# Spectral mixing and two expert layers on one Trainium2 core: split and transpose of a slot's rows two slots ahead

## The chip, the core and the metric

The kernel runs on one core of a Trainium2 chip. The metric is the device time of one execution in microseconds; the median of three runs before the change is 3485.12 us (3482.34 to 3485.62). Five engines work side by side: TensorE (PE, with its weight loads listed as PEld), VectorE (DVE), ScalarE (ACT), GpSimd (POOL) and SyncE (SP), which here issues DMAs only. Each engine takes its instructions in the order in which the program lists them.

## The reference

What is computed, cut to what matters:

```python
X = np.fft.fft(np.fft.fft(x, axis=1), axis=2)      # x: 8 x 3072 x 256
x = X.real.reshape(24576, 256)
h = x @ w_in                                       # 256 -> 2048
x = softplus(h) @ w_out                            # 2048 -> 256
xn = x / (norm(x) + 1e-6); en = emb / (norm(emb) + 1e-6)
logits = xn @ en.T / tau                           # 8 experts
e = argmax(logits); gate = softmax(logits)[e]
out = gate * (relu(x @ w1[e]) @ w2[e])             # 256 -> 1024 -> 256, expert e of each row
```

## The kernel before, in words

**First stage** (until about 2330 us of the span). The transform and the dense layer run as one software pipeline over 256 units (batch, tile, quarter of the features). A router gives each finished row an expert, and POOL scatters the rows into `bucket` in DRAM, sorted by expert (line 960).

**Second stage.** `phase2` (it works under the name P2) runs 104 slots of rows that share one expert. A slot has 256 rows, as two tiles of 128 rows; the last 8 slots have one tile. All matmuls use f16 pairs (a high and a low part), so each product is three matmuls. One slot j is made of these steps, and each step is a small function:

- `p2_load` (line 1126): SP loads the slot's rows `r` from `bucket`, four buffers. A load waits until the scatter of the slot that last used the buffer has landed.
- `p2_norm` (lines 1144 to 1170), a generator with four parts. Part 1: ACT squares and sums the rows (`jk`, line 1144), POOL takes the root (`nr`, line 1147). Part 2: DVE makes the power-of-two scales `s2` of the slot (lines 1150 to 1155). Part 3: DVE lines 1157 to 1160, then ACT's exponentials `lg` (line 1164). Part 4: DVE makes the output scale `gm` (lines 1167 to 1170).
- `p2_wcopy` (line 1135): from slot 19 on, DVE copies the expert's weights out of the table `W` into one of three buffers `wb`; the copy takes 2.30 us.
- `p2_split` (lines 1179 and 1180): DVE scales the rows by `s2` and splits them into a high and a low f16 part `xs`. There is one buffer `xs`.
- `p2_tr` (line 1187): SP issues one DMA that transposes `xs` into `xT`, of which there are two buffers.
- `p2_m1` (line 206 under the names `psH<-xT,wb`), called for the two halves of the features: 24 matmuls each, ACT takes relu of the sums to `hh` (line 1209), DVE the rest to `hl` (line 1210).
- `p2_m2`: 48 matmuls `psO<-wb,hh` and `psO<-wb,hl` with `hh` and `hl`, ACT scales the result to `ot` (line 1233), POOL scatters it to the output (line 1235).

The order in which a slot's turn lists them is written out by hand: load of row j+3; first half of m1(j); split and transpose of slot j+1; second half of m1(j); norm part 1 of slot j+2; weight copy for j+2; the other parts of that norm; m2(j).

In the turns in which the table `W` is filled, `ahead()` is called three times a turn: a block of zeros to `bucket` (`zt`, line 1113) and three pieces of `W` of 512 KB each (line 1116), all on SP. Of these, two pieces stand ahead of the transpose of a turn and one behind it. After the last unit of the first stage a drain begins, in which steps of P2 (one between two `yield`s) are woven into the remaining work of the first stage, three a pass; after four passes one step goes with each turn of a loop that ends the router and its scatters. The table is opened after that.

Of the kernel before, what the change touches and what calls it, by code (L numbers as in the profile page):

```python
# [142 lines left out]
def fft_moe_moe(ctx, tc, x, w_in, w128, w_out, emb, tau, w1, w2, fa, db, mcs, tid, ident, tri, misc, out,  # L143
# [832 lines left out]
    nslot = EARLY + NPS + E if P2ON else EARLY + 1  # L976
# [130 lines left out]
    def p2_zero(n):  # L1107
        if n < E:
            r0 = SY.value_load(p2["cuu"].bitcast(I32)[0:1, 2, n:n + 1], min_val=0, max_val=E * CAP - 256)
            rows = bucket[ds(r0, 128), :]  # L1110
        else:
            rows = bucket[E * CAP + (n - E) * 128:E * CAP + (n - E + 1) * 128, :]
        SY.dma_start(rows, p2["zt"])

    def p2_weights(e, q):
        SY.dma_start(p2["W"][:, e, q * 2048:(q + 1) * 2048], wsc[e][:, q // 2, q % 2 * 2048:(q % 2 + 1) * 2048])
# [4 lines left out]
    def p2_load(j):  # L1121
        rows = p2["a"].tile([128, 2, RW], F32, tag="r", name="r", bufs=RB)
        r = p2["row0"] + j * SLOT if j < K0 else p2["row1"] + (j - K0) * SLOT if j < EARLY else SY.value_load(p2["ti"][0:1, 1, j - EARLY:j - EARLY + 1],
                                                                 min_val=0, max_val=E * CAP)
        nt = 2 if j < EARLY + NPS else 1
        SY.dma_start(rows[:, 0:nt, :], bucket[ds(r, nt * 128), :].rearrange("(t p) d -> p t d", p=128))
        S2[j] = dict(rows=rows, nt=nt)

    def p2_wcopy(j):
        if j < EARLY:  # L1130
            WB[j] = p2["wb"][0 if j < K0 else -1]
            return
        r = V.value_load(p2["ti"][0:1, 0, j - EARLY:j - EARLY + 1], min_val=0, max_val=E - 1)
        WB[j] = wb = p2["wb"][(j - EARLY) % 3]
        V.tensor_copy(wb.bitcast(I32), p2["W"].bitcast(I32)[:, ds(r, 1), :].rearrange("p o n -> p (o n)"))
# [38 lines left out]
    def p2_split(j):  # L1174
        rows = S2[j]["rows"]
        xs = p2["a"].tile([128, 2, 2, 256], F16, tag="xs", name="xs", bufs=1)
        s2 = S2[j]["s2"]
        for t in range(S2[j]["nt"]):
            V.tensor_scalar(xs[:, t, 0, :], rows[:, t, 0:256], s2[:, 0, t:t + 1], None, op0=ALU.mult)
            V.scalar_tensor_tensor(xs[:, t, 1, :], rows[:, t, 0:256], s2[:, 0, t:t + 1], xs[:, t, 0, :],  # L1180
                                   op0=ALU.mult, op1=ALU.subtract)
        S2[j]["xs"] = xs

    def p2_tr(j):
        xs, nt = S2[j]["xs"], S2[j]["nt"]
        S2[j]["xT"] = xT = p2["a"].tile([128, 2, 2, 2, 128], F16, tag="xT", name="xT")
        SY.dma_start_transpose(out=xT[:, 0:nt].rearrange("p t a c n -> p (t a c) n"),
                               in_=xs[:, 0:nt].rearrange("p t a d -> p (t a d)"))

    def p2_m1(j, hf):  # L1190
        d = S2[j]
        wb, xT, nt = WB[j], d["xT"], d["nt"]
        n = nt * 128
        hh = p2["a"].tile([128, 4, 256], F16, tag=f"hh{hf}", name=f"hh{hf}", bufs=1)
        hl = p2["a"].tile([128, 4, 256], F16, tag=f"hl{hf}", name=f"hl{hf}", bufs=1)
        for q in range(4):
            f = 4 * hf + q
            if q % 2 == 0:
                ps = psH[hf % len(psH)].tile([128, 2, 256], F32, tag="H", name="psH", bufs=2)
            i = 0  # L1200
            for c in range(2):
                for a, w in ((0, 0), (0, 1), (1, 0)):
                    o = w * 2048 + c * F2 + f * 128
                    mm(ps[:, q % 2, 0:n].rearrange("p (t n) -> p t n", n=128), wb[:, o:o + 128], xT[:, 0:nt, a, c, :],
                       i == 0, i == 5)
                    i += 1
            if q % 2:
                h2, l2, p_ = hh[:, q - 1:q + 1, 0:n], hl[:, q - 1:q + 1, 0:n], ps[:, :, 0:n]
                A.activation(h2, p_, AF.Relu)  # L1209
                V.scalar_tensor_tensor(l2, p_, 0.0, h2, op0=ALU.max, op1=ALU.subtract)  # L1210
        d[f"h{hf}"] = (hh, hl)

    def p2_m2(j):
        d = S2.pop(j)
        wb, rows, nt = WB.pop(j), d["rows"], d["nt"]
        gm = d["gm"]
        ps = {}
        for hf, t in ((0, 0), (0, 1), (1, 0), (1, 1)):
            if t >= nt:
                continue  # L1220
            hh, hl = d[f"h{hf}"]
            if hf == 0:
                ps[t] = psO[0].tile([128, 256], F32, tag="O", name="psO", bufs=2)
            for q in range(4):
                f = 4 * hf + q
                ts_ = slice(t * 128, (t + 1) * 128)
                o = 4096 + f * 256
                mm(ps[t], hh[:, q, ts_], wb[:, o:o + 256], f == 0, False)
                mm(ps[t], hh[:, q, ts_], wb[:, o + 2048:o + 2304], False, False)
                mm(ps[t], hl[:, q, ts_], wb[:, o:o + 256], False, f == 7)  # L1230
            if hf:
                ot = p2["a"].tile([128, 256], F32, tag="ot", name="ot", bufs=2)
                A.activation(ot, ps[t], AF.Copy, scale=gm[:, t:t + 1])  # L1233
                G.memset(gap, 0.0)
                no_dep(G.indirect_dma_start(  # L1235
                    out=out, out_offset=bass.IndirectOffsetOnAxis(ap=rows.bitcast(I32)[:, t, 264:265], axis=0),
                    in_=ot, in_offset=None, bounds_check=NTOK - 1, oob_is_err=False), "out")

    def phase2():
        p2_wcopy(0)  # L1240
        p2_wcopy(1)
        for j in range(min(2, nslot)):
            for _ in p2_norm(j):
                yield
        p2_split(0)
        yield
        p2_tr(0)
        yield
        todo = None

        def ahead():
            for fn in todo.pop(0) if todo else ():
                fn()

        for j in range(nslot):
            if todo is None and "W" in p2:
                todo = [[] for _ in range(4 * E + 1)]
                table = p2_table()
                for t in todo[:-1]:
                    t.append(lambda: next(table, None))  # L1260
                for n in range(E + 2):
                    todo[3 * n].append(lambda n=n: p2_zero(n))
                for n in range(4 * E):
                    todo[n].append(lambda n=n: p2_weights(n // 4, n % 4))
                todo[-1].append(lambda: V.tensor_copy(p2["W"].bitcast(F32)[:, :, 4096], kall))
            if j == EARLY - RB + 1:
                for _ in table:
                    pass
            for n in range(len(S2) + j, min(j + RB, nslot)):
                p2_load(n)  # L1270
            ahead()
            p2_m1(j, 0)
            yield
            ahead()
            if j + 1 < nslot:
                p2_split(j + 1)
                p2_tr(j + 1)
            p2_m1(j, 1)
            yield
            ahead()  # L1280
            if j + 2 < nslot:
                nrm = p2_norm(j + 2)
                next(nrm)
                while j + 2 >= EARLY and todo:
                    ahead()
                p2_wcopy(j + 2)
                for _ in nrm:
                    pass
            p2_m2(j)
            yield  # L1290

    P2 = phase2()
    cur = [0]

# [310 lines left out]
```

## Time and profile before

| what | value |
|---|---|
| median of 3 runs | 3485.12 us |
| the profiled execution, its own time | 3496.98 us |
| its span | 3495.2 us |
| TensorE busy | 3078.9 us (88%) |
| VectorE busy | 2796.1 us (80%) |
| ScalarE busy | 2260.5 us (65%) |
| GpSimd busy | 2138.7 us (61%) |

The profiled execution was 11.86 us longer than the median of the runs. Busy shares are averages over two stages with different limits, so the second stage is read by stretches: from the start of m1 of slot 0 (2333.45 us), of slot 5 (2396.73), of slot 18 (2585.19) and of slot 96 (3426.14) to the end. The first stretch holds the drain, the second the loading of the table, the third 78 equal slots, and the last the 8 half slots. PEclk is the granted clock of TensorE as a share of 2.4 GHz; the other level is half of it.

### The profile page before, as it was taken

The numbers are of one execution on the slowest core, as the hardware profiler recorded it, in microseconds if no ns is written. First come the engines' busy times: TensorE is split into PE (matmuls) and PEld (weight loads), VectorE is DVE, ScalarE is ACT, GpSimd is POOL, SyncE is SP. The second block draws the span as 40 slices with busy tenths as digits, with TensorE's granted clock in tenths as the row PEclk, the third lists the DMA queues.
The fourth block names the chain that finished last, engine by engine and source line by source line (L and its number), as shares of the span: only waits on it lengthen the run. The fifth ranks groups of instructions, "written<-read, shape, count | busy, mean of one in ns | idle before, by whom it ended". The sixth has DMA issues, their size and how long they took to land.

```text
span 3495.2 us, 76414 instructions
## 1 busy us (share of the span) xinstructions
PE 3078.9 (88%) x31264; PEld 2740.8 (78%) x31264; DVE 2796.1 (80%) x4488; ACT 2260.5 (65%) x3400; POOL 2138.7 (61%) x1855
## 2 busy tenths in 40 slices
PE   3788898888987988888988999998889999999997
PEld 3677787876876877777887899877778888888886
DVE  7779898988888989988988988984557777777776
ACT  5777777767877878867877888763344444444443
POOL 5357677776786777777777787662234444444443
PEclk8899998998999999999999999999899999999999
DMA  4111210311211211211111000114643333332221
GB/s 138 48 49 53 71 57 28 101 40 38 73 52 51 80 42 62 80 46 51 50 46 31 19 17 20 65 38 107 175 117 76 75 75 80 75 75 74 73 73 38
DMA packets 197088, 223.74 MB, mean 64 GB/s; under 512 B 119028, under 2 KB 154751, under 8 KB 196480
## 3 DMA queue, kind: packets, MB, share of 16 engines
q1 hardware_dynamic: 177920, 167.32, 18.1%
q0 software_dynamic: 18816, 51.54, 4.2%
q8 instruction: 244, 4.00, 0.5%
q14 instruction: 108, 0.88, 0.1%
HBM read 122.91 MB, written 70.71 MB: 55 GB/s over the span
## 4 chain that ended last, share of the span: by engine, by line
issue 29%; PE 24%; DVE 20%; POOL 12%; ACT 10%; DMA 4%; POOLq 0%; SPq 0%; DVEq 0%; ACTq 0%
PE G L206 12%; DVE e L836 5%; PE pu L206 4%; POOL out_dram L1235 3%; DVE gl L860 3%; PE pv L206 3%; ACT e L831 2%; POOL gh L847 2%; ACT e L827 2%; DVE h L814 2%; DVE h L813 2%; PE psb L206 2%; PE psH L206 1%; ACT e L822 1%; POOL xt L495 1%
## 5 line engine op out<-in xcount | busy, mean ns | idle before, releaser
L847 POOL TENSOR_SCALAR gh<-e,sc 128x1536 f16<-128x1536 f32 (+1 forms) x256 | 620.8, 2425 | 493.5 <-DVE e L836 333.2
L206 PE MATMUL G<-wo_s,gh 128*128 128x264 f16 x6144 | 832.7, 284 | 2.2 <-POOL gh L850 2.0
L206 PEld LDWEIGHTS <-gh 128*128 128x128 f16 x6144 | 602.7, 101 | 100.2 <-POOL gh L850 3.3
L206 PE MATMUL psH<-xT,wb 128*128 128x256 f16 (+1 forms) x4992 | 560.3, 274 | 67.1 <-DMA xT<-xs 66.5
L836 DVE SCALAR_TENSOR_TENSOR e<-h,e 128x1536 f32<-128x1536 f32 x256 | 531.6, 2077 | 75.3 <-ACT e L831 71.8
L206 PEld LDWEIGHTS <-wb 128*128 128x128 f16 x4992 | 480.2, 100 | 137.7 <-DMA xT<-xs 78.3
L206 PEld LDWEIGHTS <-win_s 128*128 128x128 f16 x6144 | 534.0, 100 | 24.6 <-DVE h L814 11.6
L206 PE MATMUL psO<-wb,hh 128*128 128x256 f16 x3200 | 529.8, 273 | 0.6 <-ACT hh L1209 0.6
L206 PE MATMUL G<-wo_s,gl 128*128 128x264 f16 x3072 | 440.3, 281 | 28.6 <-DVE gl L860 28.4
L1147 POOL TENSOR_TENSOR nr<-ssq,half 128x2 f32<-128x2 f32 (+1 forms) x104 | 237.5, 2284 | 355.3 <-ACT jk L1144 355.0
L860 DVE SCALAR_TENSOR_TENSOR gl<-e,sc,gh 128x1536 f16<-128x1536 f32 (+1 forms) x256 | 451.0, 1762 | 3.6 <-POOL gh L847 2.2
L206 PE MATMUL psO<-wb,hl 128*128 128x256 f16 x1600 | 436.2, 273 | 0.6 <-DVE hl L1210 0.5
L1209 ACT ACTIVATE hh<-psH 128x512 f16<-128x512 f32 (+1 forms) x416 | 239.6, 579 | 269.7 <-PE psH L206 263.8
L1210 DVE SCALAR_TENSOR_TENSOR hl<-psH,hh 128x512 f16<-128x512 f32 (+1 forms) x416 | 268.7, 666 | 181.4 <-ACT hh L1209 173.3
L822 ACT ACTIVATE e<-h 128x1536 f32<-128x1536 f32 x256 | 378.0, 1477 | 47.7 <-DVE h L814 46.7
L1235 POOL DMA_INDIRECT out_dram<-ot,r x200 | 202.3, 1011 | 311.2 <-ACT ot L1233 272.3
L831 ACT ACTIVATE e<-e 128x1536 f32<-128x1536 f32 x256 | 379.5, 1482 | 4.0
L827 ACT ACTIVATE e<-e 128x1536 f32<-128x1536 f32 x256 | 378.4, 1478 | 0.0
L206 PE MATMUL pu<-pqh,win_s 128*128 128x192 f16 (+1 forms) x2048 | 371.6, 251 | 3.8 <-ACT h L806 3.8
L206 PEld LDWEIGHTS <-gl 128*128 128x128 f16 x3072 | 303.3, 100 | 89.0 <-DVE gl L860 38.5
L206 PEld LDWEIGHTS <-hh 128*128 128x128 f16 x3200 | 312.6, 98 | 36.8 <-ACT hh L1209 0.7
L813 DVE SCALAR_TENSOR_TENSOR h<-pv,sc,h 128x768 f32<-128x768 f32 (+1 forms) x256 | 258.7, 1011 | 99.2 <-ACT h L806 50.5
(274 smaller groups left out, 5902.8 us busy)
## 6 DMA issues: line engine op xcount, KB each, us to landing
xt<-in_x_dram SPq DMA_DIRECT2D x114, 384.0 KB
r<-bucket SPq DMA_DIRECT2D x96, 268.0 KB
wt<-in_w_dram SPq DMA_DIRECT2D x16, 1024.0 KB
wsc<-wo SPq DMA_DIRECT2D x32, 512.0 KB
W<-wsc SPq DMA_DIRECT2D x32, 512.0 KB
raw<-in_w_in_dram SPq DMA_DIRECT2D x8, 512.0 KB
raw<-in_w_out_dram SPq DMA_DIRECT2D x8, 512.0 KB
wb<-wsc SPq DMA_DIRECT2D x2, 2048.0 KB
```

The source lines that it names most:

```text
L206: T.matmul(o, l, r, start=start, stop=stop)
L813: V.scalar_tensor_tensor(h[:, :, n:384], pv[:, :, s0:n], sc["ninv"], h[:, :, s0:n], op0=ALU.mult, op1=ALU.add)
L822: A.activation(e, h, AF.Abs)
L827: A.activation(e, e, AF.Exp, scale=-1.0)
L831: A.activation(e, e, AF.Ln, bias=1.0)
L836: V.scalar_tensor_tensor(flat(d["e"]), flat(d["h"]), 0.0, flat(d["e"]), op0=ALU.max, op1=ALU.add)
L847: G.tensor_scalar(gh[:, 0:n], e[:, 0:n], sg, 1.0, op0=ALU.mult, op1=ALU.mult)
L860: V.scalar_tensor_tensor(flat(d["gl"]), flat(d["e"]), scal[u[0]]["sg"], flat(d["gh"]), op0=ALU.mult, op1=ALU.subtract)
L1147: G.tensor_tensor(nr[:, 0:nt], ssq[:, 0:nt], half[:, 0:nt], op=ALU.pow)
L1209: A.activation(h2, p_, AF.Relu)
L1210: V.scalar_tensor_tensor(l2, p_, 0.0, h2, op0=ALU.max, op1=ALU.subtract)
L1235: no_dep(G.indirect_dma_start(out=out, out_offset=bass.IndirectOffsetOnAxis(ap=rows.bitcast(I32)[:, t, 264:265], axis=0), in_=ot, in_offse ...
```

## The change

```diff
@@ phase2 @@
         for j in range(min(2, nslot)):
             for _ in p2_norm(j):
                 yield
-        p2_split(0)
-        yield
-        p2_tr(0)
-        yield
+        for j in range(min(2, nslot)):
+            p2_split(j)
+            yield
+            p2_tr(j)
+            yield
         todo = None
...
             p2_m1(j, 0)
             yield
             ahead()
-            if j + 1 < nslot:
-                p2_split(j + 1)
-                p2_tr(j + 1)
             p2_m1(j, 1)
             yield
             ahead()
...
                 p2_wcopy(j + 2)
+                next(nrm)
+                p2_split(j + 2)
+                p2_tr(j + 2)
                 for _ in nrm:
                     pass
             p2_m2(j)
```

Split and transpose of slot j+1 leave the middle of m1(j). In their place the turn of slot j splits and transposes slot j+2, behind part 2 of that slot's norm and ahead of its parts 3 and 4. Slots 0 and 1 are split and transposed ahead of the loop, which takes two more steps of P2. No instruction is added or taken away, and no buffer changes.

DVE, one turn among the 78 equal slots. Here `xs` is the split, `hl` the two halves of m1's low part, `wb` the weight copy, and the rows behind it the norm of the slot two ahead. Before (the pair of `xs` rows stands twice, once for each tile of rows, and so in the second fence; it is shown once):

```order
L1210 SCALAR_TENSOR_TENSOR hl_46820<-psH,hh_46819 128x512 x2
L1179 TENSOR_SCALAR xs<-r,s_46732 128x256
L1180 SCALAR_TENSOR_TENSOR xs<-r,s_46732,xs 128x256
L1210 SCALAR_TENSOR_TENSOR hl_46859<-psH,hh_46858 128x512 x2
L1135 COPY wb_31812<-W 128x4097
L1150 TENSOR_SCALAR u<-nr 128x2
L1155 TENSOR_SCALAR s_46909<-u 128x2
L1157 TENSOR_SCALAR nr<-nr 128x2
L1160 SCALAR_TENSOR_TENSOR u<-r,nr 128x2
L1167 TENSOR_SCALAR dn<-dn 128x2
```

The same turn with the change:

```order
L1210 SCALAR_TENSOR_TENSOR hl_46827<-psH,hh_46826 128x512 x2
L1210 SCALAR_TENSOR_TENSOR hl_46859<-psH,hh_46858 128x512 x2
L1135 COPY wb_31693<-W 128x4097
L1150 TENSOR_SCALAR u<-nr 128x2
L1155 TENSOR_SCALAR s_46909<-u 128x2
L1179 TENSOR_SCALAR xs<-r,s_46909 128x256
L1180 SCALAR_TENSOR_TENSOR xs<-r,s_46909,xs 128x256
L1157 TENSOR_SCALAR nr<-nr 128x2
L1160 SCALAR_TENSOR_TENSOR u<-r,nr 128x2
L1167 TENSOR_SCALAR dn<-dn 128x2
```

The split has moved from between the two `hl` halves to between the scales `s` and line 1157; it now reads the scales of the same turn (`s_46909`) and no longer those of the turn before (`s_46732`).

SP, one turn in which the table is filled: the zero block, three pieces of `W`, the transpose, and the row load of the next turn. Before:

```order
L1113 DMA bucket<-zt 128x268
L1116 DMA W<-wsc 128x2048 x2
L1187 DMA_TRANSPOSE xT<-xs 128x8x128
L1116 DMA W<-wsc 128x2048
L1126 DMA r<-bucket 128x2x268
```

With the change:

```order
L1113 DMA bucket<-zt 128x268
L1116 DMA W<-wsc 128x2048 x3
L1187 DMA_TRANSPOSE xT<-xs 128x8x128
L1126 DMA r<-bucket 128x2x268
L1109 TENSOR_LOAD cuu
```

The transpose has moved behind the third piece of `W`, and it is now that of slot j+2 and not j+1. The first of these turns is that of slot 6 before and of slot 5 with the change, since the two steps ahead of the loop put every turn two steps of P2 later against the drain.

## Rows read from the trace of the kernel before

**Rows 1.** Busy time by stretches: span, then each engine, granted clock, DMA share, GB/s

```profile
2333.45:2396.73 63.28, 62.80 (x577) 55.72 (x575) 34.85 (x97) 25.51 (x68) 27.89 (x42) 1.00 0.32 71
2396.73:2585.19 188.46, 152.15 (x1251) 128.77 (x1249) 89.61 (x331) 63.45 (x182) 43.95 (x75) 0.89 0.57 156
2585.19:3426.14 840.95, 822.48 (x7491) 730.32 (x7489) 611.56 (x1481) 372.76 (x1087) 374.61 (x390) 1.00 0.30 75
3426.14:3495.20 69.06, 47.38 (x578) 42.64 (x575) 40.78 (x115) 20.59 (x68) 24.84 (x25) 0.92 0.13 30
```

**Rows 2.** Who waited for whom: PE from 2200 us, SP's queue 2600 to 3440

```profile
PE psH L206 <- DMA xT<-xs: 66.5, 40, 9.7
...
SPq L1126 <- DMA out_dram<-ot,r: 599.3, 79, 9.1
```

**Rows 3.** Timeline of one equal slot: start, us, engine, line, instruction, idle before

```profile
2800.47 5.40 PE L206 MATMUL psH<-xT,wb 128*128 128x256 f16 x48
2800.90 0.39 ACT L1164 ACTIVATE lg<-r,u,nr 128x8 f32<-128x8 f32 x1 [3.93 <-DVE u L1160]
2802.38 0.58 ACT L1209 ACTIVATE hh<-psH 128x512 f16<-128x512 f32 x1
2805.91 0.60 ACT L1209 ACTIVATE hh<-psH 128x512 f16<-128x512 f32 x1 [0.71 <-PE psH L206]
2807.32 2.30 DVE L1135 COPY wb<-W 128x4097 int32 x1
2807.53 2.66 POOL L1147 TENSOR_TENSOR nr<-ssq,half 128x2 f32<-128x2 f32 x1 [2.81 <-ACT jk L1144]
2807.63 0.39 SPq L1126 DMA_DIRECT2D r<-bucket  x1
2808.14 1.27 SPq L1187 DMA_TRANSPOSE xT<-xs  x1
2810.78 0.16 DVE L1157 TENSOR_SCALAR nr<-nr 128x2 f32<-128x2 f32 x1
2811.37 0.39 ACT L1164 ACTIVATE lg<-r,u,nr 128x8 f32<-128x8 f32 x1 [3.93 <-DVE u L1160]
2811.85 5.41 PE L206 MATMUL psH<-xT,wb 128*128 128x256 f16 x48 [0.73 <-DMA xT<-xs]
2822.34 5.40 PE L206 MATMUL psH<-xT,wb 128*128 128x256 f16 x48
```

**Rows 4.** The split, all 104 slots: shortest, median and longest, ns

```profile
L1179 DVE TENSOR_SCALAR xs<-r,s x200: 333/346/1644, 2294.0 to 3474.3; 128x256 f16<-128x256 f32 x100
L1180 DVE SCALAR_TENSOR_TENSOR xs<-r,s,xs x200: 483/484/487, 2295.7 to 3474.8; 128x256 f16<-128x256 f32 x100
```

**Rows 5.** Timeline of SP and PE while the table is filled

```profile
2455.19 0.82 SPq L1116 DMA_DIRECT2D W<-wsc  x2
2456.12 1.62 SPq L1187 DMA_TRANSPOSE xT<-xs  x1
2457.80 0.59 SPq L1116 DMA_DIRECT2D W<-wsc  x1
2462.02 7.53 PE L206 MATMUL psH<-xT,wb 128*128 128x256 f16 x48 [4.79 <-DMA xT<-xs]
```

**Rows 6.** Timeline where the router's last scatters end: slots 5 to 7

```profile
2410.41 0.96 POOL L960 DMA_INDIRECT bucket<-rows,dst  x1 [5.53 <-DMA r<-bucket]
...
2414.59 0.39 ACT L1164 ACTIVATE lg<-r,u,nr 128x8 f32<-128x8 f32 x1 [10.88 <-DVE u L1160]
...
2433.29 6.92 PE L206 MATMUL psH<-xT,wb 128*128 128x256 f16 x36 [9.69 <-DMA xT<-xs]
```

**Rows 7.** Timeline of the half slots at the end

```profile
3465.34 0.39 ACT L1164 ACTIVATE lg<-r,u,nr 128x8 f32<-128x8 f32 x1 [3.86 <-DVE u L1160]
...
3472.46 0.39 ACT L1164 ACTIVATE lg<-r,u,nr 128x8 f32<-128x8 f32 x1 [3.87 <-DVE u L1160]
...
3479.42 4.48 PE L206 MATMUL psH<-xT,wb 128*128 128x128 f16 x48 [2.31 <-DMA xT<-xs]
```

## The prediction

> **What bounds the kernel now.** I read the busy times by stretches first, then the table of waits, then one slot in the timeline.
>
> The stretches [rows 1] show TensorE busy for 822.48 of 840.95 us in the 78 equal slots (18 to 95), at the full granted clock, and for 152.15 of 188.46 us in slots 5 to 17, at a mean clock of 0.89. What m1 and m2 of one slot need when nothing is late is the distance of two starts of m1 with no wait between: 2822.34 - 2811.85 = 10.49 us [rows 3]. So the 78 equal slots need 818.2 us and lose 22.7; the 13 slots of the second stretch need 136.4 us and lose 52.1. These two losses are what the change can reach.
>
> The table of waits [rows 2] names the owner: 66.5 us of idle TensorE, in 40 waits, end with the transposed rows `xT`. In slots 5 to 17 the idle time is 36.3 us (188.46 - 152.15), and the other 15.8 of the 52.1 are matmuls at the lower of the clock's two levels: behind a wait of 4.79 us m1 took 7.53 us [rows 5] instead of 5.40 [rows 3].
>
> The slot in the timeline [rows 3] shows why `xT` is late. The transpose issues at 2808.14 and m1 starts at 2811.85, 3.71 us later, though m1 could have started 0.89 us earlier (11.38 - 10.49). The split ends near 2806.2, so the transpose lost about 2 us behind the row load, which issues at 2807.63 on the same queue. That load waits for the scatter of the slot that last had its buffer, 599.3 us in 79 waits [rows 2].
>
> **The equal slots.** The transpose now has a full slot more. Counted from a start of m1, part 2 of the norm ends at about 10.3 us (line 1157, the next in order, starts at 2810.78). The split is two pairs of a median 0.346 and 0.484 us [rows 4], 1.66 us in all, so it ends near 12.0. With 3.71 us to land, `xT` is there at 15.7 and is wanted at 20.98. Its buffer is free at 5.4, when m1 of the same turn ends. The row load now stands behind the transpose, where it has time: its rows are squared a full slot later.
>
> What pays is ACT. `lg` waits for DVE lines behind the split, and behind `lg` queue the scaling `ot` of the slot before and the four `hh` of the next. Its loop before [rows 3]: from the last `hh` (2805.91) to `lg` (2811.37) 5.46 us, from `lg` to the first `hh` (2800.90 to 2802.38) 1.48, from first to last `hh` three times 0.60 at most. With the split's 1.66 that is 10.40 us, against 10.49 that TensorE needs. It fits, by 0.09 us; below it, m2 still has about 1 us before it needs the later `hh` and `hl`. POOL's root ends with the weight copy (2807.32 + 2.30, the root 2807.53 + 2.66), and the copy starts no later than now, since the split is no longer ahead of it. Bounds: all of the 22.7 us back if the loop holds; a loop longer by 0.3 us than counted makes the slot 10.70 and adds 16, so 6 back. I take 19 back, nearer to the loop as its rows give it.
>
> **Slots 5 to 17.** The split comes before weight copies exist here (they start two turns ahead of slot 19), so the ACT loop is shorter by the copy and no bound. What decides is the DMA queue. Alone, the transpose takes 3.71 us to land [rows 3]. Behind two pieces of `W` it took 5.90 (2456.12 to 2462.02) [rows 5]. Now three stand ahead of it; a third piece adds half of that difference, 1.1 us, or, counted from the issue of the first piece (2462.02 - 2455.19 = 6.83), half of 6.83 - 3.71, 1.6 us, so it lands within 7.5 us of its issue at about 10 us of the turn, near 17.5, and is wanted at 20.98. DMA engines were 57% busy here; 13 slots in 147 us instead of 188.46 would make that 73%.
>
> The Trainium skill, "DMA: Bandwidth & Descriptors", section "Queues, rings and completion order", says that each DMA engine takes its descriptors in ring order and that a completion counts only after every earlier write of that engine. That speaks against this edit, and the two landing times, 3.71 and 5.90 us, agree with it; by it alone the transpose would pay for all three pieces each time.
>
> One stop stays. The router's last scatters on POOL wait for a row load [rows 6], which holds the norm's root behind them, so `lg` waited 10.88 us until 2414.59. The change makes that worse by the split, 1.66, and shows about 5 us that the `xT` wait has hidden so far. So I leave 6 us for it, and 5 for rest waits behind `W`: 52.1 - 11 = 41 back. Bounds: 46 (only the stop stays) and 20 (the table keeps more than half of the loss).
>
> **The drain.** Two more steps of P2 stand ahead of the loop, so the 48 matmuls of slot 0's m1 (5.40 us, [rows 3]) come later against the first stage's last units. TensorE was busy for 62.80 of 63.28 us here [rows 1], so they may leave a hole now and be paid behind it: between 0 and 6 us, I take 3. The order of the drain's scatters on POOL is the same but for that shift.
>
> **The half slots.** Their pace is `lg` to `lg`, 7.12 us [rows 7], a loop of DVE, POOL and ACT with matmuls of half the size. It gets one tile's split, 0.83 us, in six turns, up to 5 us more, but the split leaves DVE ahead of the copy for the same time. The last two slots have no norm behind them, so slot 103's `xT` is there early: its wait of 2.31 us goes, and m1 at 4.48 us instead of half of 5.40 gives up to 1.7 more. I take 4 back; bounds 8 back and 5 lost.
>
> **The sum.** 3 - 41 - 19 - 4 = -61 us, made against the profiled execution, whose own time of 3496.98 us is 11.86 above the median. I carry it over to the median unreduced: 3485.12 - 61 = 3424. The outermost ends are 0 - 46 - 23 - 8 = -77 (3408) and 6 - 20 - 6 + 5 = -15 (3470).
>
> **The rivals.**
>
> The table's DMAs eat the lead. There is one buffer `xs`, so the split of the next slot waits until the transpose has landed. If that comes later than about 19 us of its turn, the wait goes from DVE to `lg` and to m1. The 57% and the row load that follows each transpose speak for it, the 3 us of slack against. It would keep half of the stretch's loss: 26 back instead of 41, so 3424 + 15 = 3439.
>
> The lead is not there: if the scales come late in every turn, the transpose stays as late as it is now. The root ends 0.6 us ahead of line 1157 in [rows 3], a full slot ahead of the need, so I see only the turns of [rows 6]. It would give 3485 and the drain's 3 us, 3488.
>
> Slower: the ACT loop becomes the bound. It has 0.09 us to spare, and the split's first operation took 1644 ns at its worst against a median of 346 [rows 4]. If one of its two in each slot is that slow, the loop is 10.40 + 1.30 = 11.70, 1.21 us above TensorE, 94 us in 78 slots instead of the 22.7 lost now. That is +71 in the place of -19: 3 - 41 + 71 - 4 = +29, so 3514. It decides from a slot of 11.32 us, where 78 slots lose the 65 us that cancel the rest. Against it: behind the root, POOL's next work in order is the scatter of `ot`, which waits for `lg`, so it is idle while the split runs.
>
> **How the numbers follow.** Forecast 0.67, the table's DMAs 0.18, no lead 0.05, slower 0.08, and 0.02 for a loop just over TensorE that keeps part of the gain. The range of 3406 to 3452 holds the forecast with its bounds near the low end and the table's rival; it leaves out the other cases and the outer ends of the bounds. About 0.2% (7 us) is what a measurement of this kernel can tell from no change. Faster by more: 0.67 + 0.18 + 0.02 = 0.87. Within it: the 0.05 of no lead. Slower: 0.08.
>
> **What would show it.** In the profile after, TensorE's waits for `xT` should fall from 66.5 to under 10 us. The equal slots should start every 10.49 us, with `lg` some 2 us behind the start of m1 where it is 0.43 now (2800.90 - 2800.47). In slots 5 to 17 the clock should stay near full level, and POOL's stop of about 5 us should be the one long wait left. I am wrong if the slots start further apart than 10.7 us with TensorE waiting for `hh` or `hl`, if DVE's split waits for the transpose, or if the drain grows by over 6 us.

## The result and the profile after

The kernel with the change takes 3444.80 us (median of 4 runs, 3440.48 to 3448.18), the kernel before beside it 3485.37 (4 runs, 3482.34 to 3495.64). The ratio, estimated from all the runs and so not quite that of the two medians, is 0.9878, 95% interval 0.9855 to 0.9901: 42.5 us less, 34.5 to 50.5. Forecast were 61 us less, so the sign was right and a third of the gain did not come.

The busy time by stretches, columns as in [rows 1], from the start of m1 of slots 0, 5, 18 and 96:

```profile
2330.65:2391.67 61.02, 60.10 (x553) 53.38 (x551) 33.50 (x96) 24.14 (x67) 23.41 (x39) 1.00 0.30 76
2391.67:2558.76 167.09, 145.98 (x1251) 124.64 (x1249) 91.00 (x330) 60.32 (x182) 44.02 (x74) 0.95 0.70 175
2558.76:3376.19 817.43, 817.43 (x7490) 732.68 (x7488) 620.52 (x1481) 353.18 (x1086) 376.70 (x390) 1.00 0.31 77
3376.19:3438.70 62.51, 44.71 (x578) 39.56 (x575) 40.45 (x117) 18.91 (x68) 26.48 (x25) 0.95 0.15 34
```

| stretch | before | after | change | forecast |
|---|---|---|---|---|
| slots 0 to 4 (the drain) | 63.28 | 61.02 | -2.3 | +3 |
| slots 5 to 17 (the table) | 188.46 | 167.09 | -21.4 | -41 |
| 78 equal slots, 18 to 95 | 840.95 | 817.43 | -23.5 | -19 |
| half slots | 69.06 | 62.51 | -6.6 | -4 |
| from m1 of slot 0 to the end | 1161.75 | 1108.05 | -53.7 | -61 |

These are one execution of each kernel; of the 53.7 us that they show, 42.5 arrive in the runs (where the other 11 may be is told behind the experiments).

The table of waits from 2300 us on (us in total, times, longest), which answers to the first of [rows 2]:

```profile
PE psH L206 <- DMA xT<-xs: 14.7, 8, 3.8
...
DVE xs L1179 <- issue: 23.1, 8, 6.0
DVE xs L1179 <- DMA xT<-xs: 7.3, 2, 4.0
```

TensorE's waits for `xT` fell from 66.5 us in 40 waits to 14.7 in 8, all of them in slots 8 to 16. In their place DVE now stands in front of its split for 30.4 us: 7.3 that the view puts down to the transpose, and 23.1 under "issue", for which it shows no releaser. In the timeline six of these latter eight splits start 0.03 to 0.04 us after an m1 that had waited for the same landing (the longest, 6.0 us, at 2486.86, behind m1 at 2486.82), so their cause is taken to be the same.

One equal slot, which answers to [rows 3]:

```profile
2810.18 0.35 DVE L1179 TENSOR_SCALAR xs<-r,s 128x256 f16<-128x256 f32 x1
2810.27 5.40 PE L206 MATMUL psH<-xT,wb 128*128 128x256 f16 x48
2811.90 1.25 SPq L1187 DMA_TRANSPOSE xT<-xs  x1
2812.34 0.39 ACT L1164 ACTIVATE lg<-r,u,nr 128x8 f32<-128x8 f32 x1 [5.58 <-DVE u L1160]
...
2815.71 0.60 ACT L1209 ACTIVATE hh<-psH 128x512 f16<-128x512 f32 x1 [0.33 <-PE psH L206]
2820.75 3.44 PE L206 MATMUL psH<-xT,wb 128*128 128x256 f16 x30
2822.81 0.39 ACT L1164 ACTIVATE lg<-r,u,nr 128x8 f32<-128x8 f32 x1 [5.56 <-DVE u L1160]
```

The slot takes 10.48 us (2820.75 - 2810.27) and TensorE has no idle time in it. The transpose issues 1.6 us into the turn, and `lg` starts 2.07 us behind m1 where it was 0.43. The last `hh` waits 0.33 us for its matmuls: by that ACT's loop is shorter than TensorE's work, by 0.33 us at most.

The place where the gain is missing, from m1 of slot 10 (2459.03) to that of slot 12 (2486.82), while the table is filled; it answers to [rows 5]:

```profile
2459.02 0.35 DVE L1179 TENSOR_SCALAR xs<-r,s 128x256 f16<-128x256 f32 x1 [3.34 <-DMA xT<-xs]
2459.03 7.07 PE L206 MATMUL psH<-xT,wb 128*128 128x256 f16 x48 [1.99 <-DMA xT<-xs]
2461.19 0.39 ACT L1164 ACTIVATE lg<-r,u,nr 128x8 f32<-128x8 f32 x1 [8.07 <-DVE u L1160]
2461.96 0.81 ACT L1233 ACTIVATE ot<-psO,gm 128x256 f32<-128x256 f32 x2
2464.04 0.97 POOL L1235 DMA_INDIRECT out_dram<-ot,r  x1 [0.20 <-issue]
2471.74 0.42 SPq L1126 DMA_DIRECT2D r<-bucket  x1
2472.42 0.35 DVE L1179 TENSOR_SCALAR xs<-r,s 128x256 f16<-128x256 f32 x1 [3.27 <-issue]
2474.60 0.35 SPq L1113 DMA_DIRECT2D bucket<-zt  x1
2475.00 1.40 SPq L1116 DMA_DIRECT2D W<-wsc  x3
2476.50 2.59 SPq L1187 DMA_TRANSPOSE xT<-xs  x1
2486.82 1.53 PE L206 MATMUL psH<-xT,wb 128*128 128x256 f16 x8 [3.78 <-DMA xT<-xs]
```

This is one chain. The transpose of slot 10 lands at 2459.0; only then may DVE split slot 11, since there is one `xs`. Behind the split `lg`, behind `lg` the scaling `ot` of slot 9, then its scatter (its second half issues at 2464.04). The load of slot 13's rows needs the buffer of slot 9's and issues when the scatter has landed, 7.7 us later (2471.74). The zero block waits for that load, the three pieces of `W` for the zero block, and the transpose of slot 12 stands behind them all: it issues at 2476.50 and lands 10.3 us later, at 2486.82. From the landing for slot 10 to that for slot 12 it took 27.8 us, where TensorE needs 21.0 for two slots.

A shorter loop lies inside it, closed by the one buffer `xs`. The split of slot 12 starts when the transpose of slot 11 has landed (2472.42) and takes 1.66 us, the queue holds its transpose for another 2.4, and the landing takes 10.3: 14.4 us from landing to landing, where a slot has 10.48. The 2.4 us are what the queue, and with it the chain above, adds to it.

The stop behind the router's last scatters is still there, one slot earlier [rows 6]:

```profile
2392.65 0.97 POOL L960 DMA_INDIRECT bucket<-rows,dst  x1 [5.06 <-DMA r<-bucket]
...
2401.01 0.39 ACT L1164 ACTIVATE lg<-r,u,nr 128x8 f32<-128x8 f32 x1 [11.14 <-DVE u L1160]
...
2403.13 0.61 PE L206 MATMUL psO<-wb,hh 128*128 128x256 f16 x2 [6.06 <-ACT hh L1209]
```

Slot 5 takes 19.6 us (its m1 starts at 2391.67, the next at 2411.25), of which 6.06 are this one wait of m2 for `hh`, which queue behind `lg`.

Half slots, `lg` to `lg` 7.05 us, against 7.12 in [rows 7], and without the waits for `xT`:

```profile
3399.36 0.39 ACT L1164 ACTIVATE lg<-r,u,nr 128x8 f32<-128x8 f32 x1 [4.71 <-DVE u L1160]
3406.41 0.39 ACT L1164 ACTIVATE lg<-r,u,nr 128x8 f32<-128x8 f32 x1 [4.71 <-DVE u L1160]
```

### The profile page after: what moved, and what is told of

The parts are those of the page before. It is cut to its first block, busy times and chain, and to the rows that moved or that the text cites. A ratio compares the mean times of both kernels' runs of the same rounds, so it can differ in the third digit from the quotient of the medians.

```text
span 3438.7 us, 76415 instructions
## 1 busy us (share of the span) xinstructions
PE 3059.5 (89%) x31264; PEld 2731.4 (79%) x31264; DVE 2800.7 (81%) x4488; ACT 2237.0 (65%) x3400; POOL 2144.2 (62%) x1855
## 4 chain that ended last, share of the span: by engine, by line
issue 28%; PE 23%; DVE 20%; POOL 13%; ACT 10%; DMA 4%; POOLq 0%; SPq 0%; DVEq 0%; another core or an unknown queue 0%; ACTq 0%
PE G L206 11%; DVE e L836 5%; PE pu L206 4%; POOL out_dram L1235 4%; DVE gl L860 3%; PE pv L206 3%; ACT e L831 3%; POOL gh L847 2%; ACT e L827 2%; DVE h L814 2%; DVE h L813 2%; PE psb L206 2%; DMA xT<-xs 2%; PE psH L206 1%; POOL bucket L960 1%
## 5 line engine op out<-in xcount | busy, mean ns | idle before, releaser
L206 PE MATMUL psH<-xT,wb 128*128 128x256 f16 (+1 forms) x4992 | 547.0, 270 | 15.6 <-DMA xT<-xs 14.7
L1164 ACT ACTIVATE lg<-r,u,nr 128x8 f32<-128x8 f32 x200 | 76.9, 385 | 583.8 <-DVE u L1160 583.8
L1210 DVE SCALAR_TENSOR_TENSOR hl<-psH,hh 128x512 f16<-128x512 f32 (+1 forms) x416 | 260.4, 665 | 81.7 <-ACT hh L1209 77.9
```

The costliest lines, as they stand in the source:

```text
L206: T.matmul(o, l, r, start=start, stop=stop)
L1164: A.activation(lg[:, t], rows[:, t, 256:264], AF.Exp, bias=u[:, 1, t:t + 1], scale=nr[:, t:t + 1], accum_out=dn[:, t:t + 1])
```

## The experiments

**Theory A:** in slots 5 to 17 the chain above is closed by two things, the one buffer `xs` with `lg` behind the split, and the transpose behind three pieces of `W`. Cut it, and 10 to 20 us more of that stretch come back. **Rival B:** the DMA engines, 70% busy there, are the bound, and cutting the chain moves nothing. **A third question** is the equal slots: is it ACT's loop with the split in it that is just short enough, or is there slack? Times of slots 5 to 17 (start of m1 of slot 5 to that of slot 18) come from one execution each; two pairs of kernels whose order is the same there differ by 1.5 us (167.09 and 168.54) and 2.1 us (144.93 and 147.05). Where an edit adds lines, the line numbers behind it are higher by as many.

### Split and transpose behind part 3 of the norm

```diff
                 next(nrm)
+                next(nrm)
                 p2_split(j + 2)
                 p2_tr(j + 2)
```

> Split and transpose of slot j+2 stand behind part 3 of the norm instead of ahead of it, so lg no longer stands behind the split; xs keeps its one buffer. Theory A: the loop is cut where lg used to wait for the split, so slots 5 to 17 fall from 167.1 us to 148 to 158 and the kernel to 3424 to 3436. The split that still waits for the transpose holds DVE, and with it hl of the next slot, so a part may stay. Rival B (the DMA engines are the bound): no change, 3440 to 3448. In the equal slots ACT's loop gets shorter by up to 1.66 us (lg 0.4 us behind the start of m1 instead of 2.1); since TensorE is never idle there, they stay at 10.48 us in both.

Measured: 3410.53 us (5 runs, 3403.65 to 3425.21), 0.9779 of before (0.9747 to 0.9812). Slots 5 to 17, and the half slots, in the stretches:

```profile
2400.62:2545.55 144.93, 137.62 (x1250) 121.45 (x1248) 90.39 (x328) 64.02 (x182) 44.63 (x74) 1.00 0.79 202
...
3362.99:3420.50 57.51, 44.65 (x578) 39.67 (x575) 38.64 (x115) 18.93 (x68) 16.25 (x25) 0.95 0.16 36
```

The 13 transposes issued in slots 5 to 17, from issue to landing (view of one line's instructions):

```profile
DMA to landing us min/median/max: 3.9/8.1/9.8
```

DVE's waits there, in the table of waits:

```profile
DVE xs L1179 <- DMA xT<-xs: 15.8, 9, 2.9
```

The row loads' waits on SP for the scatters in this stretch, in the kernel with the change:

```profile
SPq L1126 <- DMA out_dram<-ot,r: 68.5, 13, 8.3
```

and with split and transpose behind part 3:

```profile
SPq L1126 <- DMA out_dram<-ot,r: 29.5, 11, 5.4
```

Theory A holds and B falls: 22.2 us of the stretch come back with transposes that still take 8.1 us to land, and with the DMA engines at 79%. The split still waits for the transpose, 15.8 us, but `lg`, and with it the scatter and the row load, no longer stands behind it. Of the 22.2 us, 5.6 come from the router's stop (slot 5 takes 13.96 us instead of 19.58; in the kernel below that has the same order there and doubles later splits it takes 15.07). There `lg` starts 6.09 us behind m1 instead of 9.34: it no longer waits for the split, and the router's scatters come 1.6 us earlier, presumably by the same in the turn before. More than expected came back: the stretch ends below its range, and the half slots gain too, 5.0 us:

```profile
3383.17 0.39 ACT L1164 ACTIVATE lg<-r,u,nr 128x8 f32<-128x8 f32 x1 [3.99 <-DVE u L1160]
3389.51 0.39 ACT L1164 ACTIVATE lg<-r,u,nr 128x8 f32<-128x8 f32 x1 [4.01 <-DVE u L1160]
```

Their pace is 6.34 us instead of 7.05. There the loop through DVE, `lg` and `hh` is the bound, and one tile's split (0.83 us) had stood in it.

### The zero block and the pieces of W behind the transpose

```diff
             p2_m1(j, 0)
             yield
-            ahead()
...
                 p2_split(j + 2)
                 p2_tr(j + 2)
+                for _ in range(3):
+                    ahead()
```

(All three calls of `ahead()` of a turn go from their places. The steps on DVE that make the router's table, which `ahead()` lists as well, move with them.)

> The zero block and the three pieces of W of a turn are issued behind the transpose of that turn instead of ahead of it. Theory A: the transpose no longer lands behind the pieces of W (4 to 6 us after its issue instead of 8 to 10), the split's wait for it goes, and slots 5 to 17 fall from 167.1 us to 146 to 158, the kernel to 3424 to 3436. Against that the row load of the next turn now stands behind all three pieces without the transpose between: if row loads are what is late there, the stretch stays within 163 to 172 us and the kernel at 3440 to 3450 (rival B, the DMA engines as the bound, says the same).

Measured: 3424.99 us (5 runs, 3422.88 to 3428.96), 0.9818 of before (0.9791 to 0.9844). The stretch, and behind it its transposes from issue to landing:

```profile
2393.25:2543.45 150.20, 140.35 (x1251) 122.51 (x1249) 91.71 (x328) 60.36 (x182) 44.50 (x74) 0.98 0.72 195
```

```profile
DMA to landing us min/median/max: 3.1/3.6/5.7
```

Theory A again: with the transposes landing in 3.6 us the split never waits for one and TensorE has no wait for `xT` left; 16.9 us of the stretch come back. The same 512 KB pieces pass through the same DMA engines in less time. The router's stop stays (slot 5 takes 19.63 us), which the edit does not touch.

### Both

> Both edits at once: split and transpose behind part 3 of the norm, and the zero block and pieces of W behind the transpose. Theory A: the two attack the same loop, so they do not add up: slots 5 to 17 at 146 to 155 us, the kernel at 3422 to 3433. Rival B (the DMA engines are the bound): 3440 to 3450.

Measured: 3409.66 us (5 runs, 3405.92 to 3412.88), 0.9771 of before (0.9745 to 0.9798).

```profile
2394.17:2536.06 141.89, 138.21 (x1251) 122.59 (x1248) 90.50 (x328) 64.39 (x182) 44.16 (x74) 0.99 0.77 207
```

They overlap as expected: 25.2 us, not 22.2 + 16.9, if a little more than expected (141.89 us against 146 to 155). What is left above 13 x 10.48 = 136.2 us is the router's stop (slot 5 takes 15.69 us) and 0.4 us. This is the best order found, together with the one behind part 3 alone; the runs don't tell these two apart.

### A second place for the split's result

A second buffer of its own does not fit: with it the second stage would take 144.06 KB of each partition where 142.41 are left. So the odd slots from 9 to 17 borrow a weight buffer that nothing else uses before slot 20.

```diff
-        xs = p2["a"].tile([128, 2, 2, 256], F16, tag="xs", name="xs", bufs=1)
+        if j % 2 and 8 <= j < EARLY - 1:
+            xs = p2["wb"][1][:, 0:1024].rearrange("p (t a d) -> p t a d", t=2, a=2)
+        else:
+            xs = p2["a"].tile([128, 2, 2, 256], F16, tag="xs", name="xs", bufs=1)
```

> The change, with a second place for the split's result in the odd slots 9 to 17: the third weight buffer, which nothing uses before the copy for slot 20. So the split of a slot no longer waits until the transpose of the slot before has landed; lg stays behind the split and the transposes stay behind the pieces of W. If the one buffer is the link that closes the loop: DVE's waits of xs (30.4 us in 10 waits) go to under 5 us, lg's waits in slots 5 to 17 fall by about as much, and the stretch falls from 167.1 us to 148 to 158, the kernel to 3426 to 3436. If the link is the late landing itself (8 to 10 us behind the pieces of W, whatever waits for it), TensorE's waits for xT stay at 10 to 15 us or grow, the stretch stays at 160 to 168 us and the kernel at 3437 to 3446.

Measured: 3434.24 us (5 runs, 3429.89 to 3439.82), 0.9837 of before (0.9810 to 0.9864). The stretch, and behind it the waits in it (the lines of the table of waits that have to do with `xs` and `xT`; `wb` is the second place):

```profile
2400.95:2558.11 157.16, 142.28 (x1250) 123.13 (x1248) 92.10 (x330) 62.23 (x182) 44.05 (x74) 0.97 0.73 187
```

```profile
PE psH L206 <- DMA xT<-wb: 5.2, 4, 2.2
...
PE psH L206 <- DMA xT<-xs: 3.3, 3, 1.6
...
DVE xs L1182 <- issue: 1.3, 1, 1.3
```

The one buffer is a link: with it open, DVE's waits in front of the split go from 30.4 to 1.3 us, and 9.9 us of the stretch come back, at the upper end of what was expected. It is not the whole: TensorE still waits 8.5 us for transposes behind `W`, and the queue now holds the transposes of slots 9 to 16 for 2.1 to 6.4 us after their split has ended, where it was 0.3 to 3.6 with the change. The order behind part 3 gives more, without a second place.

> Both: the second place for the split's result in the odd slots 9 to 17, and split and transpose behind part 3 of the norm. Against the latter alone (slots 5 to 17 in 144.9 us, with 15.8 us of DVE's xs waiting for xT and 4.0 us of TensorE): if the one buffer caused what is left there, the stretch falls to 140 to 143 us and the kernel to 3404 to 3410; if not, it stays at 144 to 146 us.

Measured: 3418.59 us (5 runs, 3411.87 to 3419.97), 0.9791 of before (0.9764 to 0.9818), the stretch in 144.52 us, against 144.93 without the second place. DVE's waits for `xT` fall from 15.8 to 2.7 us and TensorE's stay (4.7 us against 4.0). So once `lg` is ahead of the split, the buffer costs nothing that one execution shows; what is left there is the late landing and the router's stop.

### The new order from slot 19 on only

From the kernel before: turns up to that of slot 16 keep the old order.

```diff
-            if j + 1 < nslot:
+            if j + 1 < EARLY:
                 p2_split(j + 1)
                 p2_tr(j + 1)
...
+                next(nrm)
+                if j + 2 >= EARLY:
+                    p2_split(j + 2)
+                    p2_tr(j + 2)
```

> From the kernel before: slots 0 to 18 keep the old order (split and transpose one slot ahead), only slots from 19 on are split and transposed two slots ahead. If the gains of the stretches are separate: slots 5 to 17 as before (185 to 191 us), the equal slots at 10.48 us each from slot 19 or 20 on (817 to 822 us for slots 18 to 95), the half slots as with the whole change (62 to 63 us), in all 27 to 30 us less than before: 3455 to 3462. If the equal slots owe their pace to the lead that slots 5 to 17 leave behind, waits for xT stay in them and the kernel is at 3470 or more.

Measured: 3457.72 us (5 runs, 3452.41 to 3460.25), 0.9907 of before (0.9894 to 0.9920), 32.4 us less.

```profile
2390.01:2576.60 186.59, 147.86 (x1250) 126.04 (x1248) 89.52 (x330) 63.40 (x182) 43.93 (x75) 0.91 0.60 158
2576.60:3394.04 817.44, 817.44 (x7490) 732.68 (x7488) 619.67 (x1481) 353.19 (x1086) 365.22 (x390) 1.00 0.31 77
3394.04:3456.50 62.46, 46.10 (x578) 40.55 (x575) 40.40 (x117) 18.91 (x68) 26.48 (x25) 0.92 0.15 34
```

The stretches are separate: the equal slots and the half slots gain the same 23.5 and 6.6 us without any lead from slots 5 to 17, which stay as before. These two make 30.1 us of the 32.4.

### The two steps ahead of the loop alone

From the kernel before: `yield` twice behind `p2_tr(0)` and the `yield` that follows it.

> From the kernel before: only two empty steps of the second stage ahead of its loop, so that every turn stands two steps later against the drain, as with the change; split and transpose stay one slot ahead. The prediction put 3 us on this shift (0 to 6). If that holds, the way from m1 of slot 0 to m1 of slot 5 grows from 63.3 us to 64 to 69 and the kernel to 3486 to 3494. If the shift is free and the 2.3 us that the whole change saved there come from the lead, the way stays at 62.5 to 64 us and the kernel within 3480 to 3490. If the shift itself saved them, 60.5 to 62 us. The table is opened one turn earlier, so slots 5 to 17 may begin their waits one slot earlier.

Measured: 3485.32 us (12 runs, 3473.05 to 3493.26), 0.9996 of before (0.9985 to 1.0007).

```profile
2322.03:2382.79 60.76, 60.11 (x554) 53.30 (x552) 31.32 (x96) 24.56 (x67) 24.68 (x40) 1.00 0.29 76
2382.79:2563.84 181.05, 149.74 (x1251) 126.94 (x1249) 89.27 (x328) 63.87 (x182) 44.19 (x74) 0.92 0.63 162
```

The shift by itself gives the 2.3 us between m1 of slot 0 and of slot 5, so these were no effect of the lead, and the kernel as a whole does not change: 1.4 us less, between 5.2 less and 2.4 more. Yet in this one execution the way from m1 of slot 0 to the end is 12.5 us shorter than before (1149.27 instead of 1161.75), 7.4 of them in slots 5 to 17 (181.05 instead of 188.46). So of the 21.4 us that the change gains in slots 5 to 17, about 14 are left for the new order.

### The split issued twice

For slots 40 to 79 the split's two instructions are issued a second time over the same result, once in the order of the change and once with split and transpose behind part 3.

```diff
+            if 40 <= j < 80:
+                V.tensor_scalar(xs[:, t, 0, :], rows[:, t, 0:256], s2[:, 0, t:t + 1], None, op0=ALU.mult)
+                V.scalar_tensor_tensor(xs[:, t, 1, :], rows[:, t, 0:256], s2[:, 0, t:t + 1], xs[:, t, 0, :],
+                                       op0=ALU.mult, op1=ALU.subtract)
```

> The change, with the split's instructions issued twice for slots 40 to 79 (the second time over the same result). Theory (ACT's loop with the split in it is just under TensorE: in the equal slots hh3 to lg 7.10 us, lg to hh0 1.49, three hh steps 1.56 at most 1.80, about 10.15 to 10.4 of 10.48): the loop becomes 11.8 to 12.0 us in these 40 slots, 1.3 to 1.6 us above TensorE, so 53 to 63 us more than the change alone: 3498 to 3508. Rival (ACT has slack, the split's place ahead of lg does not matter): less than 10 us more, 3440 to 3455.

> The order with split and transpose behind part 3 of the norm (lg ahead of the split), with the split's instructions issued twice for slots 40 to 79. If ACT's loop is what the doubled split lengthens in the order of the change, it lengthens nothing here: lg waits for no split, and DVE has 8.0 us of work in a slot of 10.48, so 1.66 more fit: within 5 us of that order alone, 3405 to 3418. If it is DVE's own time that runs out, 40 or more us are added here too, 3450 or more.

Measured: 3502.61 us in the order of the change (4 runs, 3502.03 to 3515.53), 57.8 more than the change alone; 3412.36 us behind part 3 (4 runs, 3408.22 to 3418.37), 1.8 more than that order alone. A doubled slot in the order of the change (m1, `lg`, m2):

```profile
2874.94 5.40 PE L206 MATMUL psH<-xT,wb 128*128 128x256 f16 x48
...
2879.05 0.39 ACT L1164 ACTIVATE lg<-r,u,nr 128x8 f32<-128x8 f32 x1 [7.53 <-DVE u L1160]
...
2881.17 0.39 PE L206 MATMUL psO<-wb,hh 128*128 128x256 f16 x2 [0.82 <-ACT hh L1213]
```

and slots 40 to 79 with the split behind part 3:

```profile
2765.39:3184.50 419.11, 419.11 (x3842) 375.65 (x3840) 372.67 (x918) 190.37 (x560) 191.84 (x200) 1.00 0.35 78
```

In the order of the change a doubled slot takes 11.98 us (44 slots, 40 of them doubled, take 521.53 us from start to start) and TensorE waits for `hh`: without the 1.66 us of the second split the loop is 10.32 us, 0.16 below the 10.48 that TensorE needs. Behind part 3 TensorE is busy all the 419.11 us, with DVE at 372.67 of them. So it is the place ahead of `lg` that counts, not DVE's time.

## Why the prediction was right, and where not

**The equal slots** (forecast 19 less, measured 23.5). The mechanism was right step by step: the transpose out of the way, `lg` some 2 us behind m1 (2.07), and an ACT loop of 10.40 us by the forecast's sum, 10.32 by the doubled split. It stays below TensorE's need, so all of the loss came back. The place held its risk too: 0.16 us of slack, which a doubled split overran by 1.50 us a slot, as the rival of the longer ACT loop would have it. In the change itself nothing of that showed.

**Slots 5 to 17** (forecast 41 less, measured 21.4, of which the shift by itself gives 7.4): this is the term that was mis-sized, close to its lower bound of 20. The rival "the table's DMAs eat the lead" came instead of the forecast, in the way it named: the wait went from TensorE to DVE's split, then to `lg`, then back to m1. The step that failed is "it lands within 7.5 us of its issue at about 10 us of the turn, near 17.5". Measured by the timeline, the transposes for slots 9 to 16 landed 7.6 to 10.8 us after their issue, and they were issued 14.4 to 18.8 us into the turn, not 10. The landing was off by at most 3.3 us, the issue by 4.4 to 8.8. For slot 12 the scales were there 10.1 us into the turn; then the split waited 3.3 us for the buffer and took 1.7, and the queue held the transpose for 2.4 more. I had counted when DVE could split, and neither the split's wait for the landing before nor what SP has to do first: the queue stands at the row load, that at a scatter's landing, and that scatter at an `lg` which the change itself puts behind the split. I wrote of "the 3 us of slack" against this rival; the issue time alone had used it up. A sign that I had named for being wrong came with it: DVE's split waits for the transpose, 30.4 us. TensorE's waits for `xT` stayed at 14.7 us where I looked for under 10, and the mean clock in the stretch rose from 0.89 to 0.95 only.

The page that I set beside this term ("DMA: Bandwidth & Descriptors" of the Trainium skill, section "Queues, rings and completion order") speaks of descriptors taken in ring order. The landing times agree with it: a median of 8.1 us behind the pieces and 3.6 ahead of them. (The 3.71 us that I gave for the transpose alone were those of one issued 0.51 us behind a row load; next to 3.6 that made no difference.) The loss did not hang on the landing alone, though: with only `lg` moved the transposes still took 8.1 us, and 22.2 us of the stretch came back.

**The router's stop** (6 us left for it). It is there, 6.06 us of one wait and 9.1 us more than a slot in all; putting `lg` ahead of the split took 4.5 to 5.6 of these. The forecast named the split's 1.66 us as what makes it worse, and that was too little: without the split ahead of it `lg` came 3.25 us earlier.

**The half slots** (forecast 4 less, measured 6.6). Both parts were as named: the waits for `xT` went, and the split entered the loop. That it costs there is shown by the order behind part 3, which gives 5.0 us more.

**The drain** (forecast 3 more). Between m1 of slots 0 and 5 it is 2.3 us less, and the shift alone does that. In the kernel's whole time the shift costs between -5.2 and 2.4 us, so the sum's 3 was a little high at best, and its place was wrong.

**Median and profile.** Behind m1 of slot 0 the profiles show 53.7 us less and the runs 42.5 in all. By this working 11.2 us are lost ahead of m1 of slot 0, where one execution can't show them: its start lay between 2326.76 and 2339.93 us in eight kernels whose program is the same up to there. Done in the same way (the time from m1 of slot 0 to the end, less 1161.75, against the ratio), the shift alone loses 11.1 us ahead of m1, the new order from slot 19 on, which has no shift, 0.4 less than nothing, and the other seven kernels with the shift between 2 and 9. That fits two steps that come later in the drain and push m1 of slot 0 back; the forecast looked for the shift's price only behind it. Where ahead of m1 the time goes was not tried by itself and stays open.

Against the kernel with the shift alone, the profiles and the runs agree: 41.2 us less behind m1 of slot 0 (1149.27 to 1108.05) and 41.1 by the ratios (0.9996 to 0.9878). Of these the new order gives 14.0 us in slots 5 to 17, 21.4 in the equal slots and 6.1 in the half slots. By that count it is slots 5 to 17 alone that made 3424 too low (14.0 of the 41 forecast), and the other terms gave back a part. These are single executions, so the tenths should not be leaned on. The result lies within the range because the range was drawn to hold the rival too: 3444.80 is 21 us above the forecast and 6 above the rival's 3439.

## What to carry to other kernels

When a step is moved earlier, ask for its issue time what its queue stands at, and follow that back: here a DMA's lead was lost because the one buffer held the moved step, and because the queue's head waited, over four engines, for something behind that step itself. With one buffer between a producer and its transfer, nothing that the next rounds need should stand behind that producer on its engine; putting `lg` one part ahead of the split was worth 34 us of the medians, with the same instructions and buffers. A loop that fits by a tenth of a microsecond fits; whether it has slack is cheaply found by doubling its cheapest step in a part of the slots.

## What was not expected of the hardware

In the rows shown, POOL's short instructions end no earlier than DVE's weight copy when they meet it. In a half slot of the change the root (one element in each of 128 partitions) and then a memset of eight elements:

```profile
3401.79 2.66 POOL L1147 TENSOR_TENSOR nr<-ssq,half 128x1 f32<-128x1 f32 x1 [0.26 <-issue]
3402.11 2.30 DVE L1135 COPY wb<-W 128x4097 int32 x1 [0.18 <-issue]
3402.32 2.14 POOL L1234 MEMSET gap<- 1x8 f32 x1
```

and with the split behind part 3, where both were over before the copy began:

```profile
3385.59 0.57 POOL L1147 TENSOR_TENSOR nr<-ssq,half 128x1 f32<-128x1 f32 x1 [0.25 <-ACT jk L1144]
3386.12 0.09 POOL L1234 MEMSET gap<- 1x8 f32 x1
3386.23 2.30 DVE L1135 COPY wb<-W 128x4097 int32 x1 [0.41 <-issue]
```

The memset is recorded with 2.14 us beside the copy and with 0.09 without it, the root with 2.66 and 0.57, while the copy takes 2.30 us in both. Spans on POOL are rough, and DVE's next line starts behind the ends of all three (3404.48), so it does not show which of them it waited for. And the time of a transfer depended on what its queue had just been given: a transpose took a median of 3.6 us ahead of three 512 KB pieces and 8.1 behind them.
